# A three-stage kernel on one core: the last stage's second product reordered, its weights fetched by halves, one sum moved to a PSUM bank of its own

## The chip, the core and the metric

The kernel runs as one program on one core of a Trainium2 chip. Five engines work side by side, each with its own instruction stream: PE (the matrix engine, with its weight loads shown as PEld), DVE (vector), ACT (scalar), POOL and SP (both used here mostly to issue transfers). They wait for each other by semaphores. The metric is the time of one execution in microseconds (us), the median over runs; lower is better. What a measurement of this kernel can tell from no change is about 1%.

## The reference, cut to what matters

```python
x = attention(x, state)                   # 8 batches x (512 + 32) rows = 4352 rows of 512
e_idx = argmax(x @ w_gate)                # one of 8 experts for each row
out[mask] = gate * eom * (relu(x[mask] @ w1[e]) @ w2[e])
h = out @ w_in                            # 4352x512 @ 512x2048
g = h * clip(h + 3, 0, 6) / 6
return (g @ w_out).astype(float32)        # 4352x2048 @ 2048x512
```

Everything is float32 in effect: each operand is split into a high part (a rounded copy) and a low part (the rest), and a product is made of three matmuls, high by high, high by low and low by high.

## The kernel before, in words

There are three stages. `front` (0 to about 230 us) is the attention with the choice of experts. `early` and `moe1` (to about 609 us) run the experts over 41 slots of 128 rows: `slot_M1` multiplies by the first weights, `slot_TH` transposes the result and splits it into `hh` (a copy on ACT, L855) and `hl` (a subtraction on DVE, L856), and `slot_M2` of the slot before multiplies by the second weights. Beside that, `moe1` prepares the third stage's weights: `piece` takes them from 8-byte numbers to float32 (`convert`, eight DVE operations), forms sums of their quarters, splits them (`st`, a copy on ACT and a subtraction on DVE) and stores them to memory. Most slots hold one piece; slots 29, 31, 33 and 35 hold two, both ahead of `slot_M2` and `slot_TH` in the code. Each engine's stream follows the order in which the code is written.

`moe2` is the third stage. The 34 row tiles are taken in six blocks: five of three pairs of tiles, the last of two. Both products use a scheme of seven products of quarter matrices in place of eight (the quarters are 11, 12, 21, 22 and their sums, s2 among them); ORDER is the order of the seven, KIND the accumulator (x, v, y or z) into which each goes.

`Up` makes h, eight iterations n of seven products, each of six matmuls (128 x 384 in a three-tile block, 128 x 256 in the last). `bend` and `sums` make g's quarters and s2 out of it, into the buffers `G`, one iteration behind the products.

`Down` multiplies by `w_out`: 28 steps s, four for each of the seven products. In a three-tile block a step is 18 matmuls (two 128-row chunks u, three tiles j, three parts), in the last block 12. `split(s)` makes the step's operand `g`, of which there are three buffers: the sum of two quarters first, if the product is number 4 or 2 (steps 4 to 7 and 20 to 23, DVE, L1209 and L1211), then the high part (ACT, L1213), then the low part (DVE, L1214). `step(s)` first calls `split(s + 2)`. After steps 4 and 12 `out` copies an accumulator on to another (`fork`, L1240 and L1242), after 20 and 24 it adds two accumulators into output rows `o` (L1273, L1274), and after 27 it copies the last ones (L1280); POOL stores the rows (L1256). Four accumulators of three 256-column tiles lie in PSUM banks of 512 columns: tiles 0 and 1 of each have a bank to themselves, the third tile of v shares a bank with that of x, the third tile of z with that of y.

While a block's `Down` runs, the next block's rows are gathered, transposed (`block_T`, after steps 1 to 6) and turned into operands (`block_operands`, steps 8 to 18, part by part). The last three steps of a block's `Down` are woven into the first iteration of the next block's `Up`, and step 0 into the last iteration of its own.

`Ring` holds the weights in three places of 128 x 4096 numbers. SP fetches them one product at a time: for `Up` the weights of a whole iteration n (1792 KB), for `Down` those of one of the seven products (2048 KB). A place is asked for again when its last reader has been issued.

Of the kernel before, what the change touches and what calls it, by code (L numbers as in the profile page):

```python
# [20 lines left out]
P = 128  # L21
# [921 lines left out]
def sums(k, q, quad):  # L943
# [36 lines left out]
class Ring:  # L980


    def __init__(self, k):
        self.k, self.n, self.tiles = k, 0, {}
        self.seq = [(g, d, i) for g in range(len(HALVES)) for d, ii in ((0, range(8)), (1, ORDER)) for i in ii]

    def fetch(self):
        if self.n == len(self.seq):
            return
        k, n = self.k, self.n  # L990
        g, down, i = self.seq[n]
        pool, tag = ((k.reg, "ring"), (k.rawp, "raw0"), (k.rawp, "raw1"))[n % 3]
        w = pool.tile([P, 4096], F32R, tag=tag, name="wr", bufs=1)
        if down:
            k.nc.sync.dma_start(out=w.bitcast(F32), in_=k.wdn[i].rearrange("p u h c -> p (u h c)"))
            w = w.rearrange("p (u h c) -> p u h c", u=8, h=2)
        else:
            w = w[:, 0:3584]
            k.nc.sync.dma_start(out=w.bitcast(F32).rearrange("p (k f) -> p k f", k=2), in_=k.wup[i].rearrange("k p f -> p k f"))
            w = w.rearrange("p (k i h c) -> p k i h c", k=2, i=7, h=2)  # L1000
        self.tiles[g, down, i] = w
        self.n += 1

# [96 lines left out]
class Up:  # L1100
# [9 lines left out]
    def product(self, n, i):  # L1110
        k, b = self.k, self.b
        w, ps = k.ring.tiles[b.g, 0, n], self.bank(KIND[i], n)
        terms = [(hw, hx, d) for hw, hx in ((0, 0), (0, 1), (1, 0)) for d in range(2)]
        for m, (hw, hx, d) in enumerate(terms):
            k.nc.tensor.matmul(ps, w[:, d, i, hw, :], b.X[i][:, hx, d, :], start=i in (0, 4) and m == 0, stop=m == 5,  # L1115
                               skip_group_check=True)
# [25 lines left out]
    def run(self, lead, follow):  # L1142
        k, b = self.k, self.b
        for n in range(9):
# [35 lines left out]
            if cur:  # L1180
                self.product(n, 1)
                self.copy(n, "z", "y")
            if n == 7:
                b.down.split(0)
                b.down.split(1)


class Down:


    def __init__(self, k, b):
        self.k, self.b, self.g, self.o = k, b, {}, {}
        bk = k.bk
        self.acc = dict(
            x=[bk["x"][0][:, 0:256], bk["x"][0][:, 256:512], bk["x"][1][:, 0:256]],
            v=[bk["v"][0][:, 0:256], bk["v"][0][:, 256:512], bk["x"][1][:, 256:512]],
            y=[bk["y"][0][:, 0:256], bk["y"][0][:, 256:512], bk["y"][1][:, 0:256]],
            z=[bk["z"][1][:, 0:256], bk["z"][1][:, 256:512], bk["y"][1][:, 256:512]])

    def split(self, s):  # L1200
        if s > 27:
            return
        k, b = self.k, self.b
        v = k.nc.vector.tensor_tensor
        i, uu = ORDER[s // 4], s % 4
        of = lambda q: b.pair(q, uu)
        x = of({0: "11", 4: "11", 5: "s2", 1: "12", 6: "21", 2: "12", 3: "22"}[i])
        if i == 4:
            v(out=x, in0=x, in1=of("s2"), op=ALU.add)  # L1209
        elif i == 2:  # L1210
            v(out=x, in0=x, in1=of("s2"), op=ALU.subtract)  # L1211
        g = self.g[s] = k.wk.tile([P, 2, 768], F32R, tag="g", name="g", bufs=3)[:, :, 0:2 * b.w]
        k.nc.scalar.copy(g[:, 0], x)  # L1213
        v(out=g[:, 1], in0=x, in1=g[:, 0], op=ALU.subtract)  # L1214

    def step(self, s):
        k, b = self.k, self.b
        self.split(s + 2)
        i, uu = ORDER[s // 4], s % 4
        kind, g, w = KIND[i], self.g.pop(s), k.ring.tiles[b.g, 1, i]  # L1220
        last = s == 27 and b.g == len(HALVES) - 1
        for u, j in [(u, j) for j in range(b.ht) for u in range(2)] if last else [(u, j) for u in range(2) for j in range(b.ht)]:
            a = self.acc[kind][j]
            t = slice(b.w * u + 128 * j, b.w * u + 128 * j + 128)
            first = i in (0, 4) and uu == 0 and u == 0 and (j == 0 or j == 2 and kind == "x")
            for n, (hg, hw) in enumerate(((0, 0), (0, 1), (1, 0))):
                k.nc.tensor.matmul(a, g[:, hg, t], w[:, 2 * uu + u, hw, :], start=first and n == 0, stop=False,  # L1227
                                   skip_group_check=True)
        if uu == 3:
# [31 lines left out]
    def out(self, i):  # L1261
# [16 lines left out]
        elif i == 3:  # L1278
            for j in range(b.ht):
                nc.scalar.copy(self.o[1, j][:, 0:256], acc["z"][j])  # L1280
                self.store(1, j)


def moe2(k):
# [9 lines left out]
    for g, b in enumerate(k.blocks):  # L1294
# [27 lines left out]
        k.begin = lambda: None  # L1322
    d.out(3)

# [44 lines left out]
def moe1(k):  # L1369
# [14 lines left out]
    for t in range(2, SLOTS):  # L1384
# [10 lines left out]
        with guard(k, t - 1) if within else nullcontext():  # L1395
# [19 lines left out]
            if t == 39:  # L1415
                k.ring.fetch()
            for _ in range(PIECES.count(t)):
                piece()
# [25 lines left out]
        if t == 37:  # L1444
# [4 lines left out]
            k.ring = Ring(k)  # L1449
            k.ring.fetch()  # L1450
            for j in (0, 1):
                block_gather(k, k.blocks[0], j)
        if t == 40:
            k.ring.fetch()
            k.bk = {kind: [bank_of(k, tag, kind + "b") for tag in tags] for kind, tags in BANKS.items()}
# [62 lines left out]
def program(nc, arrays):  # L1518
# [21 lines left out]
```

## Time and profile before

| | |
|---|---|
| time, median of 3 runs (their range) | 1378.27 us (1378.27 to 1386.39) |
| the profiled execution, time / span in the trace | 1383.17 / 1381.6 us |
| PE busy | 1300.4 us, 94% of the span, 8316 matmuls |
| DVE, ACT, POOL busy | 909.9, 649.2, 209.0 us |
| mean granted clock of PE | 0.975 of full speed |
| moved by the transfers | 324.35 MB, 235 GB/s on average |

Busy PE is not PE at its best speed: a matmul that runs at half clock counts as busy all the same. The stretches in which PE waits, and who ended the wait, are listed by the trace; the clock is listed for any stretch one asks for.

### The profile page before, as it was taken

The numbers are of one execution on the slowest core, as the hardware profiler recorded it, in microseconds if no ns is written. First come the engines' busy times: TensorE is split into PE (matmuls) and PEld (weight loads), VectorE is DVE, ScalarE is ACT, GpSimd is POOL, SyncE is SP. The second block draws the span as 40 slices with busy tenths as digits, with TensorE's granted clock in tenths as the row PEclk, the third lists the DMA queues.
The fourth block names the chain that finished last, engine by engine and source line by source line (L and its number), as shares of the span: only waits on it lengthen the run. The fifth ranks groups of instructions, "written<-read, shape, count | busy, mean of one in ns | idle before, by whom it ended". The sixth has DMA issues, their size and how long they took to land.

```text
span 1381.6 us, 22873 instructions
## 1 busy us (share of the span) xinstructions
PE 1300.4 (94%) x8316; PEld 1170.2 (85%) x8316; DVE 909.9 (66%) x1607; ACT 649.2 (47%) x1161; POOL 209.0 (15%) x246
## 2 busy tenths in 40 slices
PE   8988999999989999999998999999899989999895
PEld 6766888888867787879998998999899989998795
DVE  7987598976726988545674567366746664664463
ACT  5763344453634433444554455345545544553442
POOL 1346211222102112110002000200020002001001
PEclk9998999999999999999999999999999999999998
DMA  9955677767733556646766776676587658665883
GB/s 352 358 203 139 236 232 258 243 207 241 255 108 125 198 205 215 243 168 214 265 230 214 286 262 236 221 269 248 208 289 259 234 197 304 241 244 193 333 321 136
DMA packets 87723, 324.35 MB, mean 235 GB/s; under 512 B 9713, under 2 KB 25201, under 8 KB 82097
## 3 DMA queue, kind: packets, MB, share of 16 engines
q1 hardware_dynamic: 60320, 254.45, 51.5%
q0 software_dynamic: 15824, 46.57, 10.5%
q10 hardware_dynamic: 11456, 21.78, 4.4%
q8 instruction: 67, 1.10, 0.3%
q14 instruction: 56, 0.45, 0.1%
HBM read 392.67 MB, written 60.39 MB: 328 GB/s over the span
## 4 chain that ended last, share of the span: by engine, by line
PE 43%; DVE 8%; DMA 5%; ACT 3%; issue 2%; ACTq 0%; POOLq 0%; POOL 0%; DVEq 0%
PE yb L1227 8%; PE xb L1115 6%; PE yb L1115 6%; PE zb L1115 6%; PE xb L1227 5%; PE vb L1115 3%; PE zb L1227 3%; DMA xg<-ys_dram,rowi 3%; DVE g L1214 2%; DMA wr<-wup_dram 2%; PE yp L805 2%; ACT g L1213 2%; PE hp L805 2%; DVE G L1211 1%; PE vb L1227 1%
## 5 line engine op out<-in xcount | busy, mean ns | idle before, releaser
L1214 DVE TENSOR_TENSOR g<-G,g 128x768 fp32r<-128x768 f32 (+1 forms) x168 | 152.5, 913 | 112.6 <-ACT g L1213 112.5
L1213 ACT CAST g<-G 128x768 fp32r<-128x768 f32 (+1 forms) x168 | 133.0, 798 | 154.4 <-PE yb L1227 58.1
L1227 PE MATMUL yb<-wr,g 128*128 128x256 f32 x1056 | 154.8, 298 | 18.2 <-DVE o L1274 15.3
L1227 PEld LDWEIGHTS yb<-wr,g 128*128 128x128 f32 x1056 | 144.1, 204 | 20.8 <-DVE o L1274 16.3
L1227 PE MATMUL xb<-wr,g 128*128 128x256 f32 x936 | 127.1, 284 | 8.4 <-DVE G L1135 3.0
L1227 PEld LDWEIGHTS xb<-wr,g 128*128 128x128 f32 x936 | 117.7, 188 | 11.6 <-DVE G L1135 4.0
L1134 ACT ACTIVATE r<-hs,half 128x384 f32<-128x384 f32 (+1 forms) x96 | 57.5, 599 | 132.0 <-DVE hs L1127 132.0
L1115 PE MATMUL xb<-X,wr 128*128 128x384 f32 (+1 forms) x576 | 107.0, 331 | 7.7 <-DMA wr<-wup_dram 7.7
L1115 PE MATMUL zb<-X,wr 128*128 128x384 f32 (+1 forms) x576 | 112.0, 330 | 0.0
L1115 PE MATMUL yb<-X,wr 128*128 128x384 f32 (+1 forms) x576 | 111.8, 329 | 0.0
L1115 PEld LDWEIGHTS xb<-X,wr 128*128 128x128 f32 x576 | 96.4, 188 | 10.1 <-DMA wr<-wup_dram 9.7
L837 ACT ACTIVATE h<-hp 128x512 f32<-128x512 f32 x76 | 45.0, 599 | 120.2 <-PE hp L805 117.9
L1256 POOL DMA_INDIRECT out_dram<-o,oid x34 | 34.5, 1016 | 430.7 <-DVE o L1274 328.8
L1115 PEld LDWEIGHTS zb<-X,wr 128*128 128x128 f32 x576 | 98.4, 189 | 0.3 <-ACT zb L1119 0.3
L1115 PEld LDWEIGHTS yb<-X,wr 128*128 128x128 f32 x576 | 98.1, 189 | 0.1
L1135 DVE SCALAR_TENSOR_TENSOR G<-r,hs 128x384 f32<-128x384 f32 (+1 forms) x96 | 51.5, 536 | 65.3 <-ACT r L1134 65.3
L805 PE MATMUL hp<-w00h,xh 128*128 128x512 f32 x304 | 88.2, 411 | 5.0 <-ACTq L1395 2.0
L805 PE MATMUL hp<-w00h,xl 128*128 128x512 f32 x304 | 84.8, 401 | 0.0
L805 PE MATMUL hp<-w00l,xh 128*128 128x512 f32 x304 | 83.8, 397 | 0.4 <-DVE w00l L709 0.4
L873 ACT ACTIVATE y<-yp,ci 128x512 f32<-128x512 f32 x37 | 25.5, 688 | 124.2 <-PE yp L805 118.1
L805 PE MATMUL yp<-w01h,hh 128*128 128x512 f32 x296 | 80.6, 415 | 2.8 <-ACT w01h L703 1.6
L1028 POOL DMA_INDIRECT xg<-ys_dram,rowi x34 | 33.8, 993 | 323.4 <-DVE oid L1042 191.5
(246 smaller groups left out, 2487.3 us busy)
## 6 DMA issues: line engine op xcount, KB each, us to landing
raw<-in_w_dram SPq DMA_DIRECT2D x75, 2048.0 KB
wr<-wup_dram SPq DMA_DIRECT2D x48, 1792.0 KB
wr<-wdn_dram SPq DMA_DIRECT2D x42, 2048.0 KB
wup_dram<-st SPq DMA_DIRECT2D x28, 512.0 KB
wdn_dram<-st SPq DMA_DIRECT2D x28, 512.0 KB
ys_dram<-y ACTq DMA_DIRECT2D x41, 256.5 KB
xt<-in_xt_dram SPq DMA_DIRECT2D x8, 1040.0 KB
xT<-in_xT_dram SPq DMA_DIRECT2D x16, 512.0 KB
```

Source lines behind the costliest of these rows:

```text
L805: nc.tensor.matmul(out, a, b, start=(i == 0), stop=(i == len(parts) - 1))
L837: nc.scalar.activation(h[:, 512 * f:512 * f + 512], ps[f], AF.Relu)
L873: nc.scalar.activation(y[:, 0:DM], ps, AF.Copy, scale=m)
L1028: k.nc.gpsimd.indirect_dma_start(out=x, out_offset=None, in_=k.ys[0:P * min(T + 8, SLOTS)], in_offset=bass.IndirectOffsetOnAxis(ap=k.rowi[ ...
L1115: k.nc.tensor.matmul(ps, w[:, d, i, hw, :], b.X[i][:, hx, d, :], start=i in (0, 4) and m == 0, stop=m == 5, skip_group_check=True)
L1134: k.nc.scalar.activation(r, h, AF.Relu, bias=k.half, scale=1.0 / 6.0)
L1135: k.nc.vector.scalar_tensor_tensor(out=self.b.quarter(q, n), in0=r, scalar=1.0, in1=h, op0=ALU.min, op1=ALU.mult)
L1211: v(out=x, in0=x, in1=of("s2"), op=ALU.subtract)
L1213: k.nc.scalar.copy(g[:, 0], x)
L1214: v(out=g[:, 1], in0=x, in1=g[:, 0], op=ALU.subtract)
L1227: k.nc.tensor.matmul(a, g[:, hg, t], w[:, 2 * uu + u, hw, :], start=first and n == 0, stop=False, skip_group_check=True)
L1256: ins = k.nc.gpsimd.indirect_dma_start(out=k.out, out_offset=bass.IndirectOffsetOnAxis(ap=b.ids[b.ht * h + j], axis=0), in_=self.o.pop((h, ...
```

## The change

- `Ring`: every place is used as two halves. An `Up` weight is stored in the order of the products, so that half 0 (1024 KB) holds the first four products of an iteration and half 1 (768 KB) the last three; a `Down` weight's half (1024 KB) serves two steps. A half is fetched again after its own last reader: in `Up` after `product(n, 1)` and after `product(m, 3)`, in `Down` after every second step.
- `Down`: the sum of quarters is a function of its own, `sum`, and runs one step ahead of the split, and both stand behind the step's matmuls and its `out`. The first two splits stand in `Up`'s iterations 5 and 6 and no longer both in 7.
- The third tile of z has the bank `z[0]` to itself.
- Of the next block's work, the transposes of tiles 4 and 5 come two steps later, and the operands one step later.
- In the last block, the matmuls of steps 26 and 27 are issued together, tile by tile, and each tile's last copy and store stands right behind its matmuls.
- `moe1`: in slots 29, 31, 33 and 35 the second piece stands behind `slot_M2` and `slot_TH`.

```diff
@@ sums (L963)
-            out = k.wup[4 * (q % 2):4 * (q % 2) + 4, q // 2, :, 256 * i:256 * i + 256]
+            o, d = ORDER.index(i), q // 2
+            o = 2048 + 768 * d + 256 * (o - 4) if o > 3 else 1024 * d + 256 * o
+            out = k.wup[4 * (q % 2):4 * (q % 2) + 4, :, o:o + 256]
@@ Ring
-        self.seq = [(g, d, i) for g in range(len(HALVES)) for d, ii in ((0, range(8)), (1, ORDER)) for i in ii]
+        self.seq = [(g, d, i, h) for g in range(len(HALVES)) for d, ii in ((0, range(8)), (1, ORDER)) for i in ii for h in range(2)]
...
+    def fetch(self, count=1):
...
+            w = self.places[n % 6 // 2][:, 2048 * (n % 2):2048 * (n % 2) + (2048 if down or not h else 1536)]
...
@@ Up.run
             if cur:
                 self.product(n, 1)
+                k.ring.fetch()
                 self.copy(n, "z", "y")
-            if n == 7:
-                b.down.split(0)
-                b.down.split(1)
+            if n in (5, 6):
+                b.down.split(n - 5)
@@ Down
-            z=[bk["z"][1][:, 0:256], bk["z"][1][:, 256:512], bk["y"][1][:, 256:512]])
+            z=[bk["z"][1][:, 0:256], bk["z"][1][:, 256:512], bk["z"][0][:, 0:256]])
+
+    def sum(self, s):
+        if s > 27:
+            return
+        b, uu = self.b, s % 4
+        q, op = {4: ("11", ALU.add), 2: ("12", ALU.subtract)}.get(ORDER[s // 4], (None, None))
+        if q:
+            x = b.pair(q, uu)
+            self.k.nc.vector.tensor_tensor(out=x, in0=x, in1=b.pair("s2", uu), op=op)
...
     def step(self, s):
-        self.split(s + 2)
...
+        if b.g < len(HALVES) - 1 or s < 26:
+            for u in range(2):
+                for j in range(b.ht):
+                    part(uu, u, j)
+        elif s == 27:
+            for j in range(b.ht):
+                for n in range(4):
+                    part(2 + n // 2, n % 2, j)
+                self.last(j)
+        if uu % 2:
             k.ring.fetch()
         if s in (4, 12, 20, 24):
             self.out(ORDER[s // 4 - 1])
+        self.sum(s + 3)
+        self.split(s + 2)
         for f in self.extra.get(s, ()):
             f()
@@ moe2
-                d.extra.setdefault(i + 1, []).append(lambda i=i: block_T(k, nxt, i, "t1"))
+                d.extra.setdefault(i + 1 if i < 4 else i + 3, []).append(lambda i=i: block_T(k, nxt, i, "t1"))
...
-                d.extra.setdefault(8 + i, []).append(lambda i=i: operands(i))
+                d.extra.setdefault(9 + i, []).append(lambda i=i: operands(i))
@@ moe1
-            for _ in range(PIECES.count(t)):
+            if t in PIECES:
                 piece()
...
+            if PIECES.count(t) > 1:
+                piece()
```

The order on PE at steps 20 to 22 of the first `Down` (kind y; `yb_8451` and `yb_8452` are y's two banks before, `yb_8454` and `yb_8455` the same after; `g` is the step's operand, and a row says what the instruction waits for). Before:

```order
L1227 MATMUL yb_8452<-wr_9352,g_9502 128x256 x3
L1227 MATMUL yb_8451<-wr_9352,g_9527 128x256 [waits Activation_49]
L1227 MATMUL yb_8451<-wr_9352,g_9527 128x256
L1227 MATMUL yb_8451<-wr_9352,g_9527 128x256 [waits DVE_49]
L1227 MATMUL yb_8451<-wr_9352,g_9527 128x256 x3
L1227 MATMUL yb_8452<-wr_9352,g_9527 128x256 [waits DVE_49]
L1227 MATMUL yb_8452<-wr_9352,g_9527 128x256 x2
```

Now:

```order
L1233 MATMUL yb_8455<-wr_8264,g_9522 128x256 x3
L1233 MATMUL yb_8454<-wr_8264,g_9548 128x256 [waits Activation_49]
L1233 MATMUL yb_8454<-wr_8264,g_9548 128x256
L1233 MATMUL yb_8454<-wr_8264,g_9548 128x256 [waits DVE_49]
L1233 MATMUL yb_8454<-wr_8264,g_9548 128x256 x3
L1233 MATMUL yb_8455<-wr_8264,g_9548 128x256 x3
```

In step 21 the matmuls on y's second bank waited a second time for DVE, for the sum `o` that reads z's third tile out of that bank; now they wait for nothing but the operand.

The order on DVE around steps 17 to 20 of the second `Down` (L1211 and now L1212 are the sums, L1214 and now L1221 the low parts, L1060, L1071 and now L1063, L1074 the next block's operands, L1274 and now L1292 the output sums). Before:

```order
L1211 TENSOR_TENSOR G_8523<-G_8523,G_8521 128x768
L1214 TENSOR_TENSOR g_10780<-G_8523,g_10780 128x768
L1211 TENSOR_TENSOR G_8523<-G_8523,G_8522 128x768
L1214 TENSOR_TENSOR g_10804<-G_8523,g_10804 128x768
L1274 TENSOR_TENSOR o_10825<-zb_8454,o_10825 128x256
L1274 TENSOR_TENSOR o_10828<-zb_8454,o_10828 128x256
L1274 TENSOR_TENSOR o_10831<-yb_8452,o_10831 128x256
L1211 TENSOR_TENSOR G_8523<-G_8523 128x768
L1214 TENSOR_TENSOR g_10835<-G_8523,g_10835 128x768
```

Now:

```order
L1212 TENSOR_TENSOR G_8526<-G_8526,G_8524 128x768
L1221 TENSOR_TENSOR g_10775<-G_8526,g_10775 128x768
L1063 TENSOR_TENSOR X_10778<-xraw_10337,X_10778 128x768
L1212 TENSOR_TENSOR G_8526<-G_8526,G_8525 128x768
L1221 TENSOR_TENSOR g_10801<-G_8526,g_10801 128x768
L1063 TENSOR_TENSOR X_10804<-xraw_10337,X_10804 128x768
L1292 TENSOR_TENSOR o_10825<-zb_8457,o_10825 128x256
L1292 TENSOR_TENSOR o_10828<-zb_8457,o_10828 128x256
L1292 TENSOR_TENSOR o_10831<-zb_8456,o_10831 128x256
L1212 TENSOR_TENSOR G_8526<-G_8526 128x768
L1221 TENSOR_TENSOR g_10835<-G_8526,g_10835 128x768
```

A sum and the low part behind it now belong to different steps, the two last operand parts stand between them, and the three output sums stand ahead of the low part of step 22.

The order on DVE in `moe1`, second piece of slot 29 (`quad` and `e` are the conversion, `st` the store's low part, `hl` the operand of the second product); the difference, with the other rows as they were:

```order
 L938 TENSOR_TENSOR quad<-e,d 128x512
+L856 TENSOR_TENSOR hl<-tp,hh 128x512 x2
 L956 TENSOR_TENSOR sums<-quad 128x512
 L961 TENSOR_TENSOR st<-quad,st 128x2x256
...
 L938 TENSOR_TENSOR quad<-e,d 128x512
-L856 TENSOR_TENSOR hl<-tp,hh 128x512 x2
```

`hl` has moved ahead of one whole piece.

## Rows read from the trace of the kernel before

**Rows 1.** Waits of PE, whole span: engine, line, releaser: total us, times, longest us.

```profile
PE yb L1227 <- DVE o L1274: 15.3, 5, 3.1
PE xb L1115 <- DMA wr<-wup_dram: 7.7, 5, 2.7
PE yp L805 <- DVE hl L856: 4.6, 3, 3.1
...
PE xb L1227 <- DVE G L1135: 3.0, 5, 0.6
PE xb L1227 <- ACT yb L1242: 2.7, 5, 0.6
...
PE vb L1045 <- DMA xg<-ys_dram,rowi: 2.4, 4, 0.9
PE yb L1227 <- DVE g L1214: 2.4, 6, 0.5
PE xb L1227 <- DVE g L1214: 2.0, 5, 0.4
...
PE vb L1227 <- DVE g L1214: 0.9, 4, 0.2
```

**Rows 2.** Timeline of PE, steps 21 to 23: start, us, instruction, xcount, [idle before <-releaser].

```profile
732.00 7.50 PE L1227 MATMUL yb<-wr,g 128*128 128x256 f32 x48 [3.06 <-DVE o L1274]
...
863.66 8.73 PE L1227 MATMUL yb<-wr,g 128*128 128x256 f32 x48 [3.06 <-DVE o L1274]
...
1338.07 5.92 PE L1227 MATMUL yb<-wr,g 128*128 128x256 f32 x48
```

**Rows 3.** Windows: stretch, us, five engines' busy us (x), PEclk, DMA share, GB/s.

```profile
863.70:868.70 5.00, 5.00 (x23) 5.00 (x24) 2.69 (x3) 1.66 (x2) 0.00 (x0) 0.50 0.00 0
1283.40:1287.00 3.60, 3.60 (x30) 3.60 (x31) 1.15 (x3) 0.86 (x2) 0.00 (x0) 1.00 1.03 431
```

**Rows 4.** Timeline of DVE, second `Down`, steps 18 to 22.

```profile
852.37 0.95 DVE L1060 TENSOR_TENSOR X<-xraw,X 128x768 fp32r<-128x768 f32 x1
853.24 0.95 DVE L1211 TENSOR_TENSOR G<-G 128x768 f32<-128x768 f32 x1
855.17 0.96 DVE L1214 TENSOR_TENSOR g<-G,g 128x768 fp32r<-128x768 f32 x1 [0.98 <-ACT g L1213]
...
863.19 0.41 DVE L1274 TENSOR_TENSOR o<-yb,o 128x256 f32<-128x256 f32 x1
```

**Rows 5.** Timeline of PE, last block, iteration 7 of `Up`, start of `Down`.

```profile
1309.26 0.98 PE L1115 MATMUL xb<-X,wr 128*128 128x256 f32 x6 [2.71 <-DMA wr<-wup_dram]
1310.07 1.40 PE L1115 MATMUL zb<-X,wr 128*128 128x256 f32 x6
...
1322.71 1.67 PE L1227 MATMUL xb<-wr,g 128*128 128x256 f32 x12 [0.64 <-DMA wr<-wdn_dram]
```

**Rows 6.** Timeline of SP's issues, second block (two rows), last block (two rows).

```profile
781.08 0.36 SPq L999 DMA_DIRECT2D wr<-wup_dram  x1
788.47 0.36 SPq L999 DMA_DIRECT2D wr<-wup_dram  x1
1299.07 0.36 SPq L999 DMA_DIRECT2D wr<-wup_dram  x1
1314.64 0.33 SPq L995 DMA_DIRECT2D wr<-wdn_dram  x1
```

**Rows 7.** Timeline of PE in `moe1`, slot 29.

```profile
468.56 2.12 PE L805 MATMUL yp<-w01h,hh 128*128 128x512 f32 x8
473.78 3.68 PE L805 MATMUL yp<-w01h,hl 128*128 128x512 f32 x8 [3.10 <-DVE hl L856]
```

**Rows 8.** Timeline of the end: the last copies and the last-but-one store.

```profile
1368.75 0.65 ACT L1280 COPY o<-zb 128x256 f32<-128x256 f32 x2 [3.52 <-PE zb L1227]
1369.40 0.97 POOL L1256 DMA_INDIRECT out_dram<-o,oid  x1 [1.32 <-ACT o L1280]
```

**Rows 9.** The page: GB/s in the 40 slices of the span.

```profile
GB/s 352 358 203 139 236 232 258 243 207 241 255 108 125 198 205 215 243 168 214 265 230 214 286 262 236 221 269 248 208 289 259 234 197 304 241 244 193 333 321 136
```

More of the change, by code (lines that the diff above doesn't have):

```diff
@@ L983, in __init__ @@
     def __init__(self, k):
-        self.k, self.n, self.tiles = k, 0, {}
-        self.seq = [(g, d, i) for g in range(len(HALVES)) for d, ii in ((0, range(8)), (1, ORDER)) for i in ii]
[L987 to L1002, printed above, removed]
+        self.k, self.n, self.tiles, self.places = k, 0, {}, []
+        self.seq = [(g, d, i, h) for g in range(len(HALVES)) for d, ii in ((0, range(8)), (1, ORDER)) for i in ii for h in range(2)]
+    def fetch(self, count=1):
+        k = self.k
+        for n in range(self.n, min(self.n + count, len(self.seq))):
+            g, down, i, h = self.seq[n]
+            if n in (0, 2, 4):
+                pool, tag = ((k.reg, "ring"), (k.rawp, "raw0"), (k.rawp, "raw1"))[n // 2]
+                self.places.append(pool.tile([P, 4096], F32R, tag=tag, name="wr", bufs=1))
+            w = self.places[n % 6 // 2][:, 2048 * (n % 2):2048 * (n % 2) + (2048 if down or not h else 1536)]
+            if down:
+                k.nc.sync.dma_start(out=w.bitcast(F32), in_=k.wdn[i, :, 4 * h:4 * h + 4].rearrange("p u h c -> p (u h c)"))
+                w = w.rearrange("p (u h c) -> p u h c", u=4, h=2)
+            else:
+                k.nc.sync.dma_start(out=w.bitcast(F32), in_=k.wup[i, :, 2048:3584] if h else k.wup[i, :, 0:2048])
+                w = w.rearrange("p (k i h c) -> p k i h c", k=2, h=2, c=128)
+            self.tiles[g, down, i, h] = w
+            self.n += 1
 class Block:
@@ L1111, in product @@
         k, b = self.k, self.b
-        w, ps = k.ring.tiles[b.g, 0, n], self.bank(KIND[i], n)
+        o, ps = ORDER.index(i), self.bank(KIND[i], n)
+        w, o = k.ring.tiles[b.g, 0, n, o // 4], o % 4
         terms = [(hw, hx, d) for hw, hx in ((0, 0), (0, 1), (1, 0)) for d in range(2)]
         for m, (hw, hx, d) in enumerate(terms):
-            k.nc.tensor.matmul(ps, w[:, d, i, hw, :], b.X[i][:, hx, d, :], start=i in (0, 4) and m == 0, stop=m == 5,
+            k.nc.tensor.matmul(ps, w[:, d, o, hw, :], b.X[i][:, hx, d, :], start=i in (0, 4) and m == 0, stop=m == 5,
                                skip_group_check=True)
@@ L1203, in split, with part @@
         k, b = self.k, self.b
[L1204 to L1211, printed above, removed]
+        x = b.pair({0: "11", 4: "11", 5: "s2", 1: "12", 6: "21", 2: "12", 3: "22"}[ORDER[s // 4]], s % 4)
         g = self.g[s] = k.wk.tile([P, 2, 768], F32R, tag="g", name="g", bufs=3)[:, :, 0:2 * b.w]
         k.nc.scalar.copy(g[:, 0], x)
-        v(out=g[:, 1], in0=x, in1=g[:, 0], op=ALU.subtract)
+        k.nc.vector.tensor_tensor(out=g[:, 1], in0=x, in1=g[:, 0], op=ALU.subtract)
     def step(self, s):
         k, b = self.k, self.b
-        self.split(s + 2)
         i, uu = ORDER[s // 4], s % 4
[L1220 to L1223, printed above, removed]
+        kind, w = KIND[i], k.ring.tiles[b.g, 1, i, uu // 2]
+        def part(uu, u, j):
+            g = self.g[s - s % 4 + uu]
             t = slice(b.w * u + 128 * j, b.w * u + 128 * j + 128)
@@ L1226, in step @@
             for n, (hg, hw) in enumerate(((0, 0), (0, 1), (1, 0))):
-                k.nc.tensor.matmul(a, g[:, hg, t], w[:, 2 * uu + u, hw, :], start=first and n == 0, stop=False,
-                                   skip_group_check=True)
-        if uu == 3:
+                k.nc.tensor.matmul(self.acc[kind][j], g[:, hg, t], w[:, 2 * (uu % 2) + u, hw, :], start=first and n == 0,
+                                   stop=False, skip_group_check=True)
+        if b.g < len(HALVES) - 1 or s < 26:
[8 more added lines that the diff above has]
+        if uu % 2:
             k.ring.fetch()
@@ L1279, in out, with last @@
             for j in range(b.ht):
-                nc.scalar.copy(self.o[1, j][:, 0:256], acc["z"][j])
-                self.store(1, j)
+                self.last(j)
+    def last(self, j):
+        self.k.nc.scalar.copy(self.o[1, j][:, 0:256], self.acc["z"][j])
+        self.store(1, j)
 def moe2(k):
@@ L1322, in moe2 @@
         k.begin = lambda: None
-    d.out(3)
 def early(k):
@@ L1449, in moe1 @@
             k.ring = Ring(k)
-            k.ring.fetch()
+            k.ring.fetch(2)
             for j in (0, 1):
@@ L1523, in program @@
     args["ys"] = nc.dram_tensor("ys_dram", (SLOTS * P, DM + 1), F32, kind="Internal").ap()
-    args["wup"] = nc.dram_tensor("wup_dram", (8, 2, P, 1792), F32, kind="Internal").ap()
+    args["wup"] = nc.dram_tensor("wup_dram", (8, P, 3584), F32, kind="Internal").ap()
     args["wdn"] = nc.dram_tensor("wdn_dram", (7, P, 8, 2, 256), F32, kind="Internal").ap()
```

4 lines of the change are left out of this document (2 added, 2 removed).

## The prediction

> **What bounds the kernel now.** I read the page first: PE is busy for 94% of the span, so a gain can only come out of the other 6% or out of a faster PE. Then the waits of PE [rows 1]: the reader is to see that the largest, five times 3.06 us, and seven smaller ones stand in the third stage, at places that the change touches, and one in `moe1`. Then the timeline of PE behind the largest wait [rows 2] and the clock there [rows 3]: the same 48 matmuls take 5.92 us in the last block, where no wait stands ahead, and 7.50 to 8.73 us behind each of the five waits, since TensorE's granted clock is 0.50 there, the lower of its two levels (1.2 of 2.4 GHz). So a wait of PE costs itself and a stretch at half speed behind it. Last the timelines of DVE, SP and the end [rows 4, 6, 8], for who ends those waits. The profiled execution took 1383.17 us, 4.9 above the median of 1378.27; the sum is made against 1383.17. A measurement of this kernel can tell about 1%, 14 us, from no change.
>
> **z's third tile in its own bank: 26.3 us.** In step 21 PE has the high part of its operand, and waits to write y's second bank until DVE has read z's third tile out of it: that sum ends at 863.60 [rows 4], and PE starts at 863.66 [rows 2]. With a bank of its own for that tile the matmuls need nothing but the operand. The wait goes: 5 x 3.06 = 15.3 us [rows 1]. Behind it the five stretches of 48 matmuls took 7.50, 8.73, 7.51, 8.68 and 8.61 us (first and second in [rows 2]); against 5.92 at full clock that is 41.0 - 29.6 = 11.4, of which I take 11.0, since a shorter wait may stay.
>
> It may stay because DVE is the next to be late. Before, sum, high part (ACT) and low part of a step are a chain: DVE idles 0.98 us between its sum and its low part [rows 4], so a step costs DVE about 2.8 us, and PE's step of 18 matmuls only 18 x 5.92/48 = 2.2. With the sum a step ahead that idle time is filled. Each 128 x 768 operation starts 0.87 us after the one before [rows 4]; sum, low part and operand part are 2.6 us for each of the steps 17 to 19, then three output sums (about 1.0), the sum of step 23 and the low part of 22 (0.87 each). From about 0.7 us after step 17 starts that makes 0.7 + 7.8 + 1.0 + 1.7 = 11.2 us. Step 22 wants its low part behind two matmuls, 5 x 2.16 + 0.24 = 11.0 us after step 17 starts (2.16 is 18 x 0.12, without the overlap of the last). So PE waits there for some 0.2 to 0.5 us, five times: about what the old waits of y's matmuls on the low part come to, 2.4 us [rows 1]. I set one against the other and count neither.
>
> **Weights by halves: 8.2 us.** Five waits of the last block's `Up` on its weights are 7.7 us [rows 1]; behind the longest, 2.71 us, six matmuls take 1.40 us, where twelve take 1.67 later [rows 5]; three such groups make some 1.5 us more. I leave 1 us in as a remainder. The reason is time: the weights that this wait was for were issued at 1299.07 [rows 6] and wanted at 1309.26 - 2.71 = 1306.55, 7.5 us later; half 0 now goes out when the first four products of an iteration are done and not all seven, and is needed two iterations later, which is 2 x 5.0 us there, and half 1 later still. Twice as many issues of 0.36 us [rows 6] cost nothing: SP has 2.5 us for each half even in the last block, and nothing else to do there.
>
> **Splits, forks, transposes: 11.0 us.** The first two splits in `Up`'s iterations 5 and 6 take away step 0's waits, on `G` 3.0 and on `g` 2.0 us [rows 1]. With z's bank out of the way and `out` ahead of the split, ACT's copies start about 0.8 us sooner: the 2.7 us that x's matmuls wait for the fork go [rows 1]. Behind the fork the cast of step s + 2 comes 0.9 us later; cast and low part end 2.7 us after step s starts, and step s + 2 starts after 4.3, so nothing is late. The transposes of tiles 4 and 5 wait for gathered rows, 2.4 us in four times [rows 1]; two steps (4.3 us) later the rows are there, and the longest wait was 0.9. In the last block the waits of v's matmuls on `g`, 0.9 us, go with the earlier sums [rows 1].
>
> **`moe1`: 6.2 us.** `hl` now stands ahead of the second piece. Its waits, 4.6 us in three [rows 1], go; behind the one of 3.10 us eight matmuls take 3.68 us in place of 2.12 [rows 7], another 1.6. The pieces come later by less than one slot (some 9 us), and the last of them is in slot 35 of 41, so their stores have some 50 us to `moe2`.
>
> **Tail: 0.8 us.** ACT copies only after the last matmul, and the two last stores follow [rows 8]. Tile by tile, the first of the four last stores goes 1.4 us earlier, but the last still waits for the last matmul and one copy, and PE has to wait some 0.4 us for ACT's copy of tile 0 out of the bank that it writes next. Bounds 0 and 1.5.
>
> **Sum:** 26.3 + 8.2 + 11.0 + 6.2 + 0.8 = 52.5, and 1383.17 - 52.5 = **1331 us**. If the profiled execution's 4.9 us over the median were lost everywhere alike, it would be 1326; they may as well lie in the stretches that go, so I stay at 1331. Bounds of the terms: z's bank 15.3 + 5 x 1.6 = 23.3 to 15.3 + 5 x 2.8 = 29.3; the wait at step 22 from none to 1 us five times (-2.4 to +2.6); halves 5 to 9; the 11.0 from 7 to 12; `moe1` from 2 (if the piece moved delays the next slot) to 6.5. Together some 1321 to 1344.
>
> **Rivals.**
>
> *The wait moves to DVE.* If the output sums or the operand parts hold up the low part by some 3 us instead of 0.5, a wait as long as the old one stands at step 22, again with half clock behind it, and the 26.3 are lost: 1383.2 - 26.2 = 1357. For it: DVE has no idle time left in steps 17 to 22 by the sum above. Against it: 9 of its operations would have to be 0.3 us longer than in [rows 4]. Chance 0.09.
>
> *The last block becomes bound by its transfers.* There a weight of 1835 kB is wanted each 5.0 us and one of 2097 kB each 5.8, 365 GB/s. Half transfers that reach only 304 GB/s, a good slice of the third stage in [rows 9], need 6.0 and 6.9 us: 8 x 1.0 + 7 x 1.1 = 16 us more, and the halves' 8.2 are lost: 1383.2 - 44.3 + 16 = 1355. Against it: with two whole transfers in flight the engines moved 431 GB/s [rows 3], and the first two slices ran at 352 and 358 with transfers of 512 and 1040 KB [rows 9]. Chance 0.09, two thirds of it at lower rates, which end within 1%.
>
> *Slower: each half pays a whole transfer's dead time.* The `Down` weight issued at 1314.64 ended PE's wait at 1322.71 [rows 5, 6]: 8.1 us for 2097 kB, of which 431 GB/s explains 4.9; 3.2 are not bytes. If halves paid them one after the other, an `Up` weight would need 4.3 + 6.4 = 10.7 us, where a three-tile iteration gives 7.4 (781.08 to 788.47, [rows 6]) and the last block 5.0, and a `Down` weight 11.3 where 8.6 and 5.8 are given: 5 x (8 x 3.3 + 7 x 2.7) + 8 x 5.7 + 7 x 5.5 = 311 us: 1383.2 - 44.3 + 311 = 1650. It decides where the next half starts only after the last has landed; if 4.5 us or more of a pair's 6.4 lie beside other transfers, no three-tile block is touched. Against it: the last block asks for whole weights of 8 us each 5.0 to 5.8 us, and PE waited 8.3 us in all [rows 1, 5] and not 3 us fifteen times, so transfers do overlap. Chance 0.04.
>
> The Trainium skill, "DMA: Bandwidth & Descriptors", Bandwidth, speaks against cutting transfers in half: it wants 1 MiB or more in each for three quarters of the peak, and its section on the anatomy of one DMA gives each some 2.0 us beside bytes at 436 GB/s. By its figures, back to back, an `Up` weight in halves takes an estimated 8.2 us in place of 7.4, and a `Down` weight 8.8 in place of 8.6; over all blocks (5.0 and 5.8 in the last) that is 86 us more, some 1424. The trace agrees with its rate (431 against 436) and with a dead time, but not with a sequence.
>
> *`moe1` gains nothing* (the split waits for the transposes anyway): 1337, within the range.
>
> **Chances.** Forecast with its own range 1321 to 1344: 0.76; the wait moves 0.09; bound by transfers 0.09; each half's dead time 0.04; the rest, 0.02, faster than 1321. The range 1318 to 1356 leaves out the slower rival and most of the two middle ones, 0.2 in all. Faster than 1364.5: 0.76 + 0.09 + 0.03 + 0.02 = 0.90; within 1%: 0.06; slower than 1392: 0.04.
>
> **What would show it.** In the profile after: no wait of y's matmuls on `o`, and the 48 matmuls behind near 5.9 us with the clock at 1.00 in every block; at step 22 waits on `g` of at most 0.5 us; no wait on `wup` weights of over 1 us; none on `hl` in `yp`; x's third tile no longer waiting for the fork. I am wrong if a wait of over 2 us stands at steps 20 to 23, if PE in the last block waits for weights in each iteration, or if the clock stays at 0.50 behind short waits.

## The result, and the profile after

The changed kernel takes 1320.35 us in the median of four runs (1317.45 to 1321.11), the kernel before 1381.28 (1378.27 to 1386.39, four runs); the ratio is 0.955, 95% interval 0.951 to 0.959: 61 us between the medians, 4.5% faster by the ratio. The profiled execution has a span of 1315.5 us against 1381.6, 66.1 us less, so that is the sum to be accounted for.

From the page of the changed kernel, the busy times and the clock in 40 slices:

```profile
PE 1275.1 (97%) x8316; PEld 1154.6 (88%) x8316; DVE 905.9 (69%) x1607; ACT 648.2 (49%) x1161; POOL 207.1 (16%) x246
...
PEclk9988999999999999999999999999999999999998
```

The same 8316 matmuls, but PE is busy for 25.3 us less and idle for 40.8 us less. The waits of PE in the changed kernel that answer to [rows 1], and those of the third stage:

```profile
PE yp L805 <- DVEq L735: 1.9, 1, 1.9
...
PE yb L1233 <- DVE g L1221: 1.0, 4, 0.3
...
PE zb L1119 <- ACT zb L1123: 0.7, 1, 0.7
...
PE zb L1233 <- ACT o L1301: 0.5, 1, 0.5
PE yp L805 <- DVE hl L856: 0.4, 1, 0.4
...
PE xb L1233 <- DVE g L1221: 0.2, 1, 0.2
```

Of some 37 us of waits in the third stage 2.4 are left. No wait for `o` at y, none for `wup`, `G`, the fork or gathered rows. Behind the wait at step 22 the granted clock stays at 1.00, which the timeline of PE (steps 22 and 23; first transposes of the first two `Down`s; steps 8 to 11 of the last block) and windows of the changed kernel show:

```profile
674.00 0.60 PE L1048 MATMUL vb<-ident,xg 128*128 128x128 f32 x4
...
720.22 4.34 PE L1233 MATMUL yb<-wr,g 128*128 128x256 f32 x34 [0.26 <-DVE g L1221]
...
796.39 0.60 PE L1048 MATMUL vb<-ident,xg 128*128 128x128 f32 x4
...
1274.31 5.91 PE L1233 MATMUL yb<-wr,g 128*128 128x256 f32 x48
```

```profile
720.20:724.40 4.20, 4.18 (x34) 4.18 (x35) 2.87 (x4) 2.74 (x8) 0.00 (x0) 1.00 0.76 250
...
471.10:474.70 3.60, 3.60 (x9) 2.72 (x10) 3.23 (x7) 0.00 (x0) 2.25 (x3) 0.53 0.53 152
```

The first window is step 22 at a clock of 1.00, where [rows 3] had 0.50; the second is slot 29 of `moe1`, where a stretch of half clock remains. DVE in the second `Down`, steps 19 to 22, against [rows 4]:

```profile
836.28 0.95 DVE L1063 TENSOR_TENSOR X<-xraw,X 128x768 fp32r<-128x768 f32 x1
837.15 0.95 DVE L1212 TENSOR_TENSOR G<-G 128x768 f32<-128x768 f32 x1
838.02 0.95 DVE L1221 TENSOR_TENSOR g<-G,g 128x768 fp32r<-128x768 f32 x1
838.89 0.95 DVE L1063 TENSOR_TENSOR X<-xraw,X 128x768 fp32r<-128x768 f32 x1
...
839.76 1.07 DVE L1292 TENSOR_TENSOR o<-zb,o 128x256 f32<-128x256 f32 x3
840.75 0.94 DVE L1212 TENSOR_TENSOR G<-G 128x768 f32<-128x768 f32 x1
```

Each operation starts 0.87 us after the one before, without the 0.98 us of idle time that stood ahead of each low part.

**Segments.** From the first transposes in one `Down` to those in the next (674.00 to 796.39) the trace has a ruler that the first stage does not disturb: the four segments of the changed kernel are 122.39, 122.39, 122.39 and 122.37 us, and kernels with the same third stage repeat them within 0.03 on other chips. The experiments are read by it (us; the last slot's transposes to the first `Down`; mean of the four; the last, with the last block, to the end):

| kernel | slot 40 to first `Down` | mean segment | last segment |
|---|---|---|---|
| before | 93.49 | 131.74 | 172.63 |
| changed | 91.97 | 122.39 | 151.96 |
| x1, bank back | 91.99 | 122.39 | 152.14 |
| x2, sums back | 91.96 | 126.12 | 159.96 |
| x3, bank alone | 93.50 | 129.33 | 166.99 |
| x4, sums behind the split, alone | 93.50 | 131.61 | 171.24 |
| x5, sums ahead of the split, alone | 93.50 | 126.47 | 161.33 |
| x6, as x5, and the bank | 93.49 | 124.97 | 161.73 |
| x7, halves asked for together in the code | 91.98 | 122.39 | 151.97 |
| x8, piece back | 91.99 | 122.39 | 151.99 |
| x9, splits late | 93.50 | 123.91 | 152.00 |
| x10, transposes back | 91.99 | 121.87 | 152.01 |
| x11, whole weights | 91.98 | 122.50 | 160.50 |
| x12, tail back | 91.98 | 122.39 | 152.50 |

Change against before: 1.5 + 4 x 9.35 + 20.7 = 59.6 us in the third stage, and 6.5 ahead of it.

### The profile page after: what moved, and what is told of

It reads as the page before. It is cut to its first block, busy times and chain, and to the rows that moved or that the text cites. A ratio compares the mean times of both kernels' runs of the same rounds, so it can differ in the third digit from the quotient of the medians.

```text
span 1315.5 us, 23131 instructions
## 1 busy us (share of the span) xinstructions
PE 1275.1 (97%) x8316; PEld 1154.6 (88%) x8316; DVE 905.9 (69%) x1607; ACT 648.2 (49%) x1161; POOL 207.1 (16%) x246
## 4 chain that ended last, share of the span: by engine, by line
PE 53%; issue 6%; DVE 4%; ACT 0%; POOL 0%; POOLq 0%; ACTq 0%; DVEq 0%
PE xb L1233 8%; PE xb L1119 6%; PE yb L1119 6%; PE zb L1119 6%; PE yb L1233 5%; PE yp L805 5%; PE hp L805 4%; PE zb L1233 4%; PE vb L1119 3%; PE vb L1233 2%; DVE g L1221 1%; PE vb L1048 1%; DVE G L1212 1%; DVE X L1063 1%; PE tp L853 1%
## 5 line engine op out<-in xcount | busy, mean ns | idle before, releaser
L1221 DVE TENSOR_TENSOR g<-G,g 128x768 fp32r<-128x768 f32 (+1 forms) x168 | 152.8, 912 | 78.0 <-ACT g L1220 77.2
L1233 PE MATMUL xb<-wr,g 128*128 128x256 f32 x936 | 124.2, 283 | 0.2 <-DVE g L1221 0.2
L1233 PE MATMUL yb<-wr,g 128*128 128x256 f32 x816 | 102.1, 283 | 1.0 <-DVE g L1221 1.0
L1233 PE MATMUL zb<-wr,g 128*128 128x256 f32 x816 | 100.9, 282 | 0.5 <-ACT o L1301 0.5
L1233 PEld LDWEIGHTS yb<-wr,g 128*128 128x128 f32 x816 | 99.1, 189 | 1.9 <-DVE g L1221 1.9
L1233 PEld LDWEIGHTS zb<-wr,g 128*128 128x128 f32 x816 | 99.1, 188 | 0.7 <-ACT o L1301 0.7
L1274 POOL DMA_INDIRECT out_dram<-o,oid x34 | 33.5, 985 | 387.3 <-DVE o L1292 354.2
```

Of the source, the lines that this page charges most:

```text
L1221: k.nc.vector.tensor_tensor(out=g[:, 1], in0=x, in1=g[:, 0], op=ALU.subtract)
L1233: k.nc.tensor.matmul(self.acc[kind][j], g[:, hg, t], w[:, 2 * (uu % 2) + u, hw, :], start=first and n == 0, stop=False, skip_group_check=True)
L1274: ins = k.nc.gpsimd.indirect_dma_start(out=k.out, out_offset=bass.IndirectOffsetOnAxis(ap=b.ids[b.ht * h + j], axis=0), in_=self.o.pop((h, ...
```

## Experiments: bank or sums

**x1**, the changed kernel with the bank undone:

```
-            z=[bk["z"][1][:, 0:256], bk["z"][1][:, 256:512], bk["z"][0][:, 0:256]])
+            z=[bk["z"][1][:, 0:256], bk["z"][1][:, 256:512], bk["y"][1][:, 256:512]])
```

> The changed kernel, but z's third tile shares y's second bank again. Theory of the prediction (the bank is what held PE in step 21, so it is worth the wait of 3.06 us and the half-clock stretch, five times): about 1320 + 26 = 1346 us, with five waits of y's matmuls on o of 2 to 3 us. Rival (DVE's late chain of sum, high and low part put the output sums late, and the bank only showed it; in the changed kernel's trace the three output sums end at 840.83, and the third tile of step 21 comes at about 839.80 + 0.72 = 840.52): waits of 0.3 to 0.5 us, no half clock, 1321 to 1324 us.

1316.65 us, ratio to before 0.954 (0.951 to 0.956). In its waits of PE:

```profile
PE yb L1233 <- DVE o L1292: 0.9, 4, 0.2
```

The wait of 0.26 us on `g` has become one of 0.2 us on `o`; the segments are the same. In the changed kernel the bank is worth nothing.

**x2**, the changed kernel with the sums undone:

```
-        self.sum(s + 3)
+        self.sum(s + 2)
         self.split(s + 2)
```

> The changed kernel, but each sum of quarters stands directly ahead of its split again (bank of its own kept, both still behind the step's matmuls and out). Theory of the prediction (bank decides, the sums only keep a small wait small): waits on g of up to 1 us at steps 21 to 23, 1321 to 1328 us. Rival (DVE's chain decides): DVE needs 2.8 us for a step where PE needs 2.16, so PE waits 2 to 4 us in steps 20 to 23 of each block, with half clock behind the longer ones: 1335 to 1350 us.

1342.01 us, ratio 0.973 (0.971 to 0.976): with the bank in place, 22.9 of the 59.6 us that the third stage gained are lost (4 x 3.73 + 8.0). Its waits and, of its timeline, steps 21 to 23 of the second `Down`:

```profile
PE yb L1233 <- ACT g L1220: 7.6, 6, 1.5
PE yb L1233 <- DVE g L1221: 6.4, 15, 0.5
...
PE vb L1233 <- DVE g L1221: 0.9, 4, 0.2
```

```profile
845.03 2.18 PE L1233 MATMUL yb<-wr,g 128*128 128x256 f32 x16 [0.49 <-DVE g L1221]
...
848.70 0.50 PE L1233 MATMUL yb<-wr,g 128*128 128x256 f32 x2 [1.49 <-ACT g L1220]
849.69 2.41 PE L1233 MATMUL yb<-wr,g 128*128 128x256 f32 x18 [0.49 <-DVE g L1221]
...
852.50 2.18 PE L1233 MATMUL yb<-wr,g 128*128 128x256 f32 x16 [0.39 <-DVE g L1221]
```

PE waits for the high part and then again for the low part of the same operand. These waits also have a price of their own. A window of one segment of x2, and one in its last segment:

```profile
800.38:926.50 126.12, 123.15 (x867) 122.12 (x866) 79.77 (x124) 64.22 (x113) 12.69 (x12) 1.00 0.76 259
1226.80:1230.20 3.40, 3.40 (x18) 3.40 (x18) 2.23 (x3) 1.81 (x3) 0.00 (x0) 0.50 0.47 198
```

The last segment has a stretch at half clock, so the price is read from the other four, at 1.00 throughout. Each has four recorded waits of 2.86 us in all where the changed kernel has one of 0.26, and is 3.73 us longer: three more waits cost 1.13 us beside their 2.60, or 0.38 each.

**x3**, the kernel before with the bank alone (the first diff the other way round):

> The kernel before, with nothing but z's third tile in a bank of its own. Theory of the prediction: five times 3.06 us and the half-clock stretches go, 1381 - 26 = 1355 us. Rival (DVE's chain): the wait on o goes, but the low parts of steps 22 and 23 come at the same time as before, so PE waits for g instead, some 0.4 and 1.7 us; what is gained is about 1 us of wait and part of the half clock: 1365 to 1378 us.

1365.21 us, ratio 0.989 (0.987 to 0.991). Its timeline of PE, steps 21 to 23 of the second `Down`:

```profile
856.94 2.42 PE L1227 MATMUL yb<-wr,g 128*128 128x256 f32 x18 [0.48 <-DVE g L1214]
...
859.75 2.17 PE L1227 MATMUL yb<-wr,g 128*128 128x256 f32 x16 [0.39 <-DVE g L1214]
...
862.55 0.50 PE L1227 MATMUL yb<-wr,g 128*128 128x256 f32 x2 [0.63 <-ACT g L1213]
863.55 2.18 PE L1227 MATMUL yb<-wr,g 128*128 128x256 f32 x16 [0.49 <-DVE g L1214]
```

The wait of 3.06 us is gone, and in its place PE waits at each step, one step per 2.8 us, DVE's pace. The gain, 1.1%, is 2.4 us a segment, about what the half-clock stretch behind the long wait cost (1.6 to 2.8 us).

**x4**, the kernel before with the sums a step ahead, but behind the split:

```
         self.split(s + 2)
+        self.sum(s + 3)
```

> The kernel before, with nothing but each sum of quarters a step ahead of its split (z's third tile still in y's bank, splits still ahead of the step). Theory of the prediction (bank decides): PE still waits for o in step 21, 1375 to 1381 us. Rival (DVE's chain decides): DVE reaches the output sums 2 to 3 us earlier, the wait on o shrinks to under 0.7 us and the clock stays up: 1381 - 20 to 27 = 1354 to 1361 us.

1377.24 us, ratio 0.998 (0.996 to 1.000): nothing, and not what my rival theory said. The five waits on `o` are still 2.9 us long. DVE's timeline in the second `Down`, up to the output sums, shows why:

```profile
853.32 0.95 DVE L1207 TENSOR_TENSOR G<-G 128x768 f32<-128x768 f32 x1
854.19 0.95 DVE L1060 TENSOR_TENSOR X<-xraw,X 128x768 fp32r<-128x768 f32 x1
855.25 0.96 DVE L1218 TENSOR_TENSOR g<-G,g 128x768 fp32r<-128x768 f32 x1
856.13 0.95 DVE L1207 TENSOR_TENSOR G<-G 128x768 f32<-128x768 f32 x1
858.05 0.96 DVE L1218 TENSOR_TENSOR g<-G,g 128x768 fp32r<-128x768 f32 x1 [0.98 <-ACT g L1217]
858.93 0.95 DVE L1207 TENSOR_TENSOR G<-G 128x768 f32<-128x768 f32 x1
859.80 0.75 DVE L1279 TENSOR_TENSOR o<-zb,o 128x256 f32<-128x256 f32 x2
```

DVE works in order. Where a sum stands directly ahead of its own low part, with ACT's cast between them, the idle 0.98 us stay (858.05). In the step before, an operand part of the next block stands between the two and fills that time, and still it is 2.81 us from one sum to the next (853.32, 856.13) as it is without (856.13, 858.93: 2.80): sum, cast and low part follow one another, and the next sum waits behind all three. Other work between the two is not enough; the next step's sum has to stand there.

**x5**, the same two lines in the other order, and **x6**, with the bank as well:

```
+        self.sum(s + 3)
         self.split(s + 2)
```

> The kernel before, with the sum of step s + 3 ahead of the split of step s + 2 (in x4_sums_alone it stood behind it, so that on DVE a sum and the low part of the same step were neighbours as before, with ACT's cast between them). z's third tile is in y's bank, split and sum are ahead of the step's matmuls and of out. Theory now (the chain sum, cast, low part is what makes DVE late; bank and the place of out decide only how much of the output sums PE still sees): DVE runs steps 17 to 20 without idle time, the output sums come some 1.2 to 2 us after the third tile of step 21 is due, and PE waits for o that long, five times: 1360 to 1370 us. Rival (the sums ahead are enough by themselves): no wait on o over 0.5 us, 1350 to 1355 us. Rival (sums ahead are worth nothing, as in x4_sums_alone): waits of 2.9 us on o, 1375 to 1380 us.

> As x5_sums_before_split, and z's third tile in a bank of its own. Theory now: with both, PE waits neither for o nor for the low part, at most 0.5 us at steps 21 to 23: the whole 26 us of the prediction's first term, 1378 - 26 = 1352 us, +-4. Rival (out has to stand ahead of the split too): waits on g of 1 us or more, 1358 to 1368 us.

1364.62 and 1359.44 us on a chip where the kernel before took 1397.86 (ratios 0.976, 0.973 to 0.979, and 0.973, 0.970 to 0.975), so the times expected can't be compared, but the segments can. In x5 this wait remains:

```profile
PE yb L1232 <- DVE o L1279: 4.6, 5, 1.1
```

It is 0.9 us in the mean where 1.2 to 2 was expected, and x6, with the bank, has none there and no wait on `g` at steps 21 to 23. Against before x5 gains 4 x 5.27 + 11.3 = 32.4 us in the third stage and x6 4 x 6.77 + 10.9 = 38.0. So the chain of sum, cast and low part is the cause; the bank takes away what is left if the output sums stand behind the split, and nothing if they stand ahead of it, as in the changed kernel.

## Experiments: weights, pieces, splits, transposes, tail

**x7**, which was to ask for both halves of a place when the whole is free, and **x11**, one whole transfer at that time:

```
             product(m, 3)
-            k.ring.fetch()
+            k.ring.fetch(2)
...
             product(n, 1)
-            k.ring.fetch()
...
-        if uu % 2:
-            k.ring.fetch()
+        if uu == 3:
+            k.ring.fetch(2)
```

(x11 has the same calls, each with one transfer of 1792 or 2048 KB.)

> The changed kernel, but the two halves of a place are asked for together, when the whole place is free, as the whole weight was before (the size of the transfers stays 1024 and 768 KB). Theory of the prediction (the earlier request gives the gain): waits on wup weights of 7 to 11 us in all come back in the last block, and some 2 us behind them, 1320 + 8 to 13 = 1328 to 1333 us. Rival (smaller transfers land faster by themselves): no such waits, 1318 to 1322 us.

> The changed kernel with each weight fetched in one transfer of 1792 or 2048 KB, when the whole place is free, in the changed layout in memory. x7_halves_together, with two transfers at that same time, lost nothing (segments 122.39 us, last segment 151.97 against 151.96 us), so the earlier request is not what helps. Theory now (PE needs only the first half to begin, and a transfer of half the size says sooner that it has landed): the waits on wup weights come back, 6 to 10 us in all, with the last segment at 159 to 163 us. Rival (the layout in memory or the other edits made the waits go): last segment 152 to 153 us.

x7 has no wait on `wup` at all and the changed kernel's segments (1333.84 us, ratio 0.954, 0.951 to 0.957, on the chip of x5). But it did not undo the earlier request. SP's issues of the last block's `Up` weights in the changed kernel, x7 and x11, in this order:

```profile
1199.84 48.23 SPq L1002 DMA_DIRECT2D wr<-wup_dram  x16
```

```profile
1215.32 48.23 SPq L1002 DMA_DIRECT2D wr<-wup_dram  x16
```

```profile
1200.49 49.75 SPq L1002 DMA_DIRECT2D wr<-wup_dram  x8
```

From the start of the last segment (1163.54, 1179.03 and 1161.00) the first issue comes after 36.30, 36.29 and 39.49 us, and of all 180 issues in x7 two differ from the changed kernel's by more than 0.05 us, by 0.7 and 0.3. SP issues half 0 as soon as PE is through with it, wherever the call stands among other engines' work in the code. So x7 is the changed kernel once more and tells nothing of the request.

x11, one run of 1323.40 us, does have the later request, with the whole transfer. In the changed kernel half 0 of these weights goes out 3.2 to 3.9 us ahead of half 1; x11 asks for the whole at the time of half 1 (39.49 us) and has in its waits:

```profile
PE xb L1124 <- DMA wr<-wup_dram: 5.9, 6, 2.1
```

Its last segment is 8.5 us longer. That is what the halves are worth, but x11 undoes two things: its request comes later, and PE's first product waits for all 1792 KB and not for the first 1024. Its longest wait, 2.1 us, is shorter than the 3.2 us of the earlier request, so that could be enough alone; the smaller transfer could be too. No run parts them.

**x8**, the second piece ahead of `slot_M2` and `slot_TH` again:

```
-            if t in PIECES:
+            for _ in range(PIECES.count(t)):
                 piece()
...
-            if PIECES.count(t) > 1:
-                piece()
```

> The changed kernel, but the second piece of slots 29, 31, 33 and 35 stands ahead of slot_M2 and slot_TH again. Theory of the prediction: the three waits of yp's matmuls on hl (4.6 us) come back with 1.6 us at half clock, 1320 + 6 = 1326 us. Rival (other waits of moe1 take their place, since one of 1.9 us on DVE's queue is there in the changed kernel at 471): 1320 to 1323 us.

1337.32 us, against 1333.84 of x7 on the same chip. The waits on `hl` of 3.10, 0.40 and 1.08 us come back. The changed kernel's timeline in slot 29 against [rows 7]:

```profile
471.09 3.68 PE L805 MATMUL yp<-w01l,hh 128*128 128x512 f32 x8 [1.87 <-DVEq L735]
```

The wait of 3.10 us has given way to one of 1.87 us, eight matmuls later, behind the conversion on DVE's queue, and in this execution half clock stands behind it too. From transposes to transposes slots 29, 31 and 35 take 17.43, 13.14 and 13.83 us before, 16.21, 12.49 and 12.55 now: 3.15 us, half of the 6.2 expected. Kernels with the same code here show that the half clock need not come; x11:

```profile
469.63 2.13 PE L805 MATMUL yp<-w01l,hh 128*128 128x512 f32 x8 [1.86 <-DVEq L735]
```

```profile
469.60:473.20 3.60, 3.56 (x20) 3.02 (x21) 3.18 (x7) 0.98 (x2) 2.26 (x3) 1.00 0.48 163
```

So it is in x1, x2, x7 and x12, with waits of 1.85 to 1.88 us and slot 29 at 14.6 to 14.7 us. There the edit is worth some 4.7 us.

**x9**, both first splits in iteration 7 again:

```
-            if n in (5, 6):
-                b.down.split(n - 5)
+            if n == 7:
+                b.down.split(0)
+                b.down.split(1)
```

> The changed kernel, but the first two splits of a block both stand in iteration 7 of Up again. It is read by segments: from the first transposes of one Down to those of the next the changed kernel takes 122.39 us, every time. Theory of the prediction: two waits of x's matmuls, on G and g, come back, 0.4 + 0.6 us a block: a segment of 123.4 us. Rival from the comparison of the traces (a wait costs more than its idle time, since the matmuls around it lose their overlap: step 0 took 7.95 us before and 6.42 after, for 1.0 us of recorded waits): 123.9 us.

One run, 1326.75 us. Segments 123.91, 1.52 us longer, for the two waits that its timeline has at each step 0:

```profile
1165.45 0.74 PE L1234 MATMUL xb<-wr,g 128*128 128x256 f32 x4 [0.40 <-DVE g L1222]
...
1166.79 1.70 PE L1234 MATMUL xb<-wr,g 128*128 128x256 f32 x12 [0.60 <-DVE G L1139]
```

1.00 us of recorded waits cost 1.52: the rival's number, and 0.26 for each wait. PE's matmuls overlap, a new one beginning each 0.12 us (48 in 5.91) while one takes 0.28 (a single one in this trace). The row counts idle time only from the end of the last, which leaves out 0.16; and behind each of the two waits the second matmul begins 0.22 us after the first and not 0.12, another 0.10.

**x10**, transposes and operands where they were:

```
-  setdefault(i + 1 if i < 4 else i + 3, [])
+  setdefault(i + 1, [])
...
-  setdefault(9 + i, [])
+  setdefault(8 + i, [])
```

> The changed kernel, but the transposes of tiles 4 and 5 and the operands stand where they were, two steps and one step earlier. Theory of the prediction: the waits on gathered rows come back, 0.4 to 0.9 us in four of the five blocks: segments of 122.8 to 123.3 us. Rival (operands one step earlier also relieve DVE in steps 17 to 19, or burden it): the wait on g at step 22 changes from 0.26 us, by up to 0.3 us either way. Rival (a wait costs 0.2 to 0.6 us more than its idle time): 123.0 to 123.9 us.

One run, 1315.84 us. No wait on gathered rows comes back, and the one on `g` at step 22 goes, since the operands leave steps 18 and 19 a step earlier; y's steps now run through, as its timeline shows:

```profile
837.33 8.80 PE L1233 MATMUL yb<-wr,g 128*128 128x256 f32 x72
```

Segments are 121.87 us: this part of the change costs 0.52 us each, 2.1 in all, again 0.26 beside a row of 0.26. Of the three expectations the second came true, on the wait at step 22; the waits on gathered rows did not come back. x10 is the fastest third stage of this study, by 2 us of 1316, less than the times can tell.

**x12**, steps 26 and 27 one after the other:

```
-        if b.g < len(HALVES) - 1 or s < 26:
...
+        last = s == 27 and b.g == len(HALVES) - 1
+        for u, j in [(u, j) for j in range(b.ht) for u in range(2)] if last else [(u, j) for u in range(2) for j in range(b.ht)]:
+            part(uu, u, j)
+        if last:
+            self.out(3)
```

> The changed kernel, but in the last block steps 26 and 27 are issued one after the other again, step 27 tile by tile with the copies and stores behind it. Theory of the prediction: the last segment (151.96 us) gets 0.8 us longer. Rival (the wait of 0.46 us that PE has for ACT's copy of tile 0 goes away, and the stores were never the end): 0 to 0.6 us shorter.

One run, 1318.24 us; the last segment is 0.5 us longer. The last two stores in the changed kernel, and in x12:

```profile
1302.41 0.97 POOL L1274 DMA_INDIRECT out_dram<-o,oid  x1 [1.32 <-ACT o L1301]
1304.57 0.96 POOL L1274 DMA_INDIRECT out_dram<-o,oid  x1 [1.19 <-ACT o L1301]
```

```profile
1304.09 0.97 POOL L1270 DMA_INDIRECT out_dram<-o,oid  x1 [2.77 <-ACT o L1297]
1305.37 0.97 POOL L1270 DMA_INDIRECT out_dram<-o,oid  x1 [0.31 <-issue]
```

From the start of its last segment (1163.54 and 1163.80) the last store goes 0.5 us earlier; PE's wait of 0.5 us for ACT's copy of tile 0 has taken part of what tile by tile gives.

## Why the prediction was right or wrong

The direction and the order of size were right: 1331 us forecast, 1320 measured, inside 1318 to 1356; none of the rivals came. But 1320 lies just outside the forecast's own 1321 to 1344, on the side that was given 0.02, and the bounds of the terms, added up, make 1322 to 1348. The sum was 52.5 us, the span lost 66.1. Step by step:

| step | expected | measured | by |
|---|---|---|---|
| bank, with sums; v's waits | 27.2 | 38.0 | x6 against before |
| first two splits | 5.0 | 7.6 | x9, five times 1.52 |
| fork | 2.7 | with gathered rows, 1.06 + 0.52 a segment, 6.3 | rest between x6 and x10 |
| transposes two steps later | 2.4 | -2.1 | x10 |
| weights by halves | 8.2 | 8.5 | x11 |
| `moe1` | 6.2 | 3.15 (4.7 where the clock stays up) | slots 29, 31, 35 |
| tail | 0.8 | 0.5 | x12 |
| front and `moe1` ahead of slot 28 | 0 | 3.3 | no edit acts there |

The measured terms make 65.3. The 3.3 us are of the first stages, where the traces of kernels with equal code differ as much (the last slot begins at 579.0 in x11, at 583.5 in x9), and count for nothing.

**The step that failed** is the first: that the bank frees PE, since behind it "the matmuls need nothing but the operand". The row named the output sum `o` as the releaser of 3.06 us, and I priced the wait by the edit that cuts this dependence. But x1 without the bank keeps the whole gain, x3 with nothing but the bank gets 1.1%, and x5 without the bank gets 32 us. DVE was late by then, because in each step with a sum its own chain of sum, cast and low part took 2.8 us or more, 0.98 of it idle; `o` was only what stood last in its queue. I had seen the chain and used it for the rest that would stay at step 22 (0.2 to 0.5 us forecast, 0.26 measured), not for the wait itself. That this term still had the right sign is luck in part: the change had the edit that does the work beside the one that was credited.

**The size** was too small by one price: I took a wait at its recorded idle time, and half-clock stretches beside it. At full clock a wait costs 0.26 us (x9: 0.52 for two; x10: 0.26 for one) to 0.38 us (x2: 1.13 for three) beside its row, with rows of 0.26 to 1.5 us. The third stage before has 39 such rows of waits in [rows 1]; at that price they are 10 to 15 us, and the third stage gained 13 more than its terms made (59.6 against 46.3). The price fits the rest; no run shows that it is all of it. The smallest waits show it best, in the kernel before, steps 5 and 6 of the last block:

```profile
1330.63 1.81 PE L1227 MATMUL vb<-wr,g 128*128 128x256 f32 x12 [0.22 <-DVE g L1214]
1332.67 1.84 PE L1227 MATMUL vb<-wr,g 128*128 128x256 f32 x12 [0.22 <-DVE g L1214]
```

From one to the next are 2.04 us, where twelve matmuls without a wait take 12 x 0.12 = 1.44: 0.60 us for a row of 0.22.

**Weights:** the size was right (x11); whether for the reason given, the earlier request, or for the smaller first transfer stays open, since x7 left the request where it was. The text also put all five waits in the last block; one of 0.86 us was in the second. The rival of the dead time in each half, and the rule of the Trainium skill beside it ("DMA: Bandwidth & Descriptors", Bandwidth), did not show: in the changed kernel, which runs with halves throughout, PE has no wait on weights in the third stage. Of its halves only those of 768 KB are below the 1 MiB that the rule asks for.

**Transposes:** the sign was wrong. The rows that came late before come in time in x10, at the old place. The halved weights, which no longer fill the queues with 2 MB at a time, may be why (x6, with whole weights, still has 3.2 us of those waits), but no run halves the weights and leaves all else as before, so this stays open. **`moe1`:** half to three quarters, since a wait of 1.87 us took over in slot 29, with half clock behind it in some executions. **Tail:** 0.8 against 0.5, within its bounds.

## What to carry to other kernels

The releaser that a row names is the instruction that came last, not the cause: look at how the releasing engine spent the steps ahead, and if it idled inside its own chain, put the next step's sum (the first part of its chain) between the parts, so that two chains overlap; filling the gap with other work left each step at 2.8 us (x4). A dependence cut at the end of the queue only moves the wait. Price a short wait of PE at its row and a fixed 0.26 to 0.38 us (this kernel, full clock), which doubles the shortest ones, or by the distance between equal starts with and without it. Where an edit has two effects, earlier and smaller, undo one of them before believing either, and look in the trace whether it was undone: a call that moves in the code need not move on the engine that carries it out (x7).

## What was not expected of the hardware

PE loses 0.26 to 0.38 us beside the recorded idle time at each wait, at full clock. The clock fell to 0.50 behind waits of 3.06 us in the third stage. Behind one and the same wait of 1.85 to 1.88 us in slot 29 it was 0.53 in a window of 3.6 us in the changed kernel and 1.00 in x1, x2, x7, x11 and x12; and x2, with its waits of 0.4 to 1.5 us close together, kept 1.00 through four segments and had 0.50 for 3.4 us in the fifth. So the wait before it did not decide by itself whether the clock fell.
